# Strassen pairs for blocks 3 and 4 too, and Silu instead of a gated tanh in the pairs: sparse attention and a feed-forward layer on one core

## The chip, the core and the metric

The kernel runs on one core of a Trainium2 chip. The metric is the time of one execution in microseconds of device time, as a median of several runs.

## The reference

Attention in 8 batches of 8 heads, 576 tokens, 64 features each; heads 0 to 3 see the last 32 tokens, heads 4 to 7 every 32nd token. Its output, 4608 tokens of 512 features, goes through a feed-forward layer with silu. All is float32.

```python
scores = q @ k.T / sqrt(64)                     # per batch and head
local   = (rel >= 0) & (rel < 32)               # heads 0..3, rel = i - j
strided = (rel >= 0) & (j % 32 == i % 32)       # heads 4..7
attn = softmax(where(mask, scores, -1e9)) @ v   # (8, 8, 576, 64)
x = attn.transpose(0, 2, 1, 3).reshape(4608, 512)
h = x @ w_in                                    # 512 x 2048
out = (h / (1 + exp(-h))) @ w_out               # 2048 x 512
```

## The kernel before

**Numbers.** Every float32 operand of the feed-forward layer is split into an upper and a lower part in a short float format (fp32r). A product is three matmuls: upper x upper, upper x lower, lower x upper.

**Blocks.** The 4608 tokens are nine blocks of 512, 0 to 8. Block 0 prepares the weights while it computes, by a list written out by hand (PLAN). Block 1 runs plain products in 16 steps. Blocks 2, 3 and 4 (`for k in range(FAST, WIDE_FIRST)`) run the first layer by Strassen's scheme in Winograd's form: in each of eight steps j there are 7 products p1 to p7 of 256 columns instead of 8. Their second layer is plain: four words "0" to "3" in the order of a step stand for the outputs of the step before. Blocks 5 and 6, and 7 and 8, are joined (class `Pair`): two blocks are the two halves of Strassen's scheme, in the first layer (56 products of 512 columns, `first_product`) and in the second (56 more, `second_product`). Here operands are sums of gated values (`sums_before`), each split in two for TensorE (`second_operand`), and results are added up from kept products (`keep`, `finished_out`).

**Sums of weights.** Sums of the weights that the scheme needs are made once, GpSimd for the first layer's (`sum_weights`, in block 1) and VectorE for the second's (`sum_outs`, at the steps in OUT_SUMS, blocks 2 to 4), and kept in DRAM. Products read them through a ring of six, in pairs eight, tiles in SBUF; `stream_on` issues the next load behind the product that frees a tile. All loads and stores of this part are issued by SyncE, in one queue.

**Attention bursts.** The attention of batches 2 to 7 comes in 18 bursts. A burst is two groups, a local and a strided one: TensorE computes the scores of the group after next and the values of this group; then come ScalarE's copies of the values, VectorE's peaks, ScalarE's exps (L529), VectorE's total, scale and transposes, and ScalarE's copies of turned blocks (`turn_across`, L602). The next burst needs what this one has softened. BURSTS says at which step (k, j) one stands. In the blocks a burst holds the four PSUM banks "ps"; in a pair's first layer it takes the banks "po".

**Silu.** Everywhere it is h (1 + tanh(h/2)) / 2: tanh on ScalarE, a `scalar_tensor_tensor` on VectorE for the gating (L1986 in pairs), and the half at the end. Tanh and exp use the same table of ScalarE.

**Order.** From block 1 on, each instruction or small group is a `job` with an engine, a cost, the jobs it follows and the places it takes from rings of buffers. `in_order` gives each job a due time backwards from PE's queue and simulates the engines; PE takes its jobs as written, the other engines choose among the first LOOK jobs, within GRAIN of the earliest start, the one due first. The order found is the program's order on each engine; semaphores make the waits on the chip. The names that the change touches are BURSTS, the orders of words, `job`, `in_order`, `sum_outs`, `burst_jobs`, `finish`, `second_operand`, `sums_before` and `run`; The UNITS (buffers of 128x512 for gated values) and GOPS (places for split operands) lie in SBUF that earlier stages have left.

## Time and profile before

| | us |
|---|---|
| median of 3 runs (820.23 to 820.51) | 820.31 |
| the profiled execution | 824.26 |
| its span, first to last instruction | 822.0 |
| PE matmuls busy | 811.3 (99%) |
| VectorE (DVE) busy | 638.5 (78%) |
| ScalarE (ACT) busy | 557.5 (68%) |
| GpSimd (POOL) busy | 74.3 (9%) |

The mean granted TensorE clock is 0.996 of full speed; it is below only in the slice from 20 to 40 us (0.83). The queue that SyncE issues moves 180.82 MB. A busy time is a union of intervals: two instructions that overlap on one engine count once, and a matmul's end is modelled. Idle time on an engine that nothing waits for costs nothing, so shares alone do not name the bound; the waits and the chain do.

### The profile page before, as it was taken

Reading aid. Unit: us, or ns where it says so; the run is one execution under the profiler, and the core shown is the slowest. Engines: PE = TensorE matmul, PEld = TensorE weight load, DVE = VectorE, ACT = ScalarE, POOL = GpSimd, SP = SyncE. Lnnn points to the kernel's source line nnn. Section 1 sums busy time; section 2 is a strip of 40 time slices with the busy share of each in tenths; the row PEclk is TensorE's granted clock in tenths of the full one; section 3 lists DMA queues with packets and bytes.
Section 4 is the critical chain, followed back from the end, with each engine's and each line's share of the span. In section 5 each row is a group of like instructions: output and inputs, shape, how many; then the busy total and the mean of one; then the engine's idle time right before and its main releaser. Section 6 shows DMA issues by size and latency. Waiting matters only on the chain.

```text
span 822.0 us, 19441 instructions
## 1 busy us (share of the span) xinstructions
PE 811.3 (99%) x7041; PEld 686.5 (84%) x7041; DVE 638.5 (78%) x1571; ACT 557.5 (68%) x1560; POOL 74.3 (9%) x122
## 2 busy tenths in 40 slices
PE   8899999999999999999999999999999999999998
PEld 5688878888898889898988888888888888888887
DVE  6799897787677778786778779676799964789754
ACT  7799876566687678777787769887555624545551
POOL 6300003784000000000000000000000000000000
PEclk9899999999999999999999999999999999999999
DMA  8787354566787876888677877876667697767676
GB/s 270 254 276 253 111 187 127 203 222 237 265 266 252 263 243 210 250 265 264 198 234 247 264 241 242 256 203 181 194 191 219 193 238 227 194 196 194 192 217 156
DMA packets 139007, 182.78 MB, mean 222 GB/s; under 512 B 29408, under 2 KB 82272, under 8 KB 138912
## 3 DMA queue, kind: packets, MB, share of 16 engines
q1 hardware_dynamic: 137392, 180.82, 71.4%
q8 instruction: 56, 0.92, 0.5%
q10 hardware_dynamic: 1520, 0.72, 0.3%
q14 instruction: 39, 0.32, 0.1%
HBM read 142.70 MB, written 38.80 MB: 221 GB/s over the span
## 4 chain that ended last, share of the span: by engine, by line
PE 97%; POOL 1%; issue 1%; DVE 0%; POOLq 0%
PE ps L1549 33%; PE po L779 27%; PE po L2103 13%; PE ps L720 11%; PE ps L2103 4%; PE ps L635 3%; PE po L2232 1%; PE ps L471 1%; PE ps L462 1%; PE po L620 0%; PE po L635 0%; POOL v L399 0%; POOL mask_strided L240 0%; POOL mask__94 L240 0%; PE po L554 0%
## 5 line engine op out<-in xcount | busy, mean ns | idle before, releaser
L1549 PE MATMUL ps<-xop,w 128*128 128x256 f32 (+1 forms) x1152 | 185.5, 310 | 0.0
L1549 PEld LDWEIGHTS ps<-xop,w 128*128 128x128 f32 x1152 | 165.6, 190 | 16.3
L529 ACT ACTIVATE sm<-sm,sums 128x54 f32<-128x54 f32 (+2 forms) x320 | 109.2, 346 | 3.5 <-DVE sums L511 3.4
L720 PE MATMUL ps<-xop,w 128*128 128x512 f32 x384 | 96.5, 400 | 0.0
L1549 PE MATMUL ps<-w,w 128*128 128x512 f32 x384 | 93.7, 389 | 0.0
L779 PE MATMUL po<-w,ghi 128*128 128x512 f32 x280 | 87.1, 392 | 0.0
L720 PEld LDWEIGHTS ps<-xop,w 128*128 128x128 f32 x384 | 72.8, 192 | 15.8
L1549 PEld LDWEIGHTS ps<-w,w 128*128 128x128 f32 x384 | 72.0, 188 | 14.9
L764 DVE TENSOR_TENSOR glo<-th,ghi 128x512 fp32r<-128x512 f32 x80 | 59.3, 743 | 12.4 <-ACT ghi L760 10.5
L529 ACT ACTIVATION_READ_ACCUMULATOR sm<-sm,sums 128x1 f32 x320 | 61.4, 192 | 0.0
L779 PEld LDWEIGHTS po<-w,ghi 128*128 128x128 f32 x280 | 50.4, 189 | 8.9 <-ACT ghi L760 0.2
L760 ACT CAST ghi<-th 128x512 fp32r<-128x512 f32 x78 | 48.3, 621 | 11.8 <-DVE th L752 7.0
L779 PE MATMUL po<-w,glo 128*128 128x512 f32 x140 | 54.6, 390 | 0.0
L779 PE MATMUL po<-stage,ghi 128*128 128x512 f32 x160 | 50.5, 397 | 0.0
L2103 PE MATMUL po<-stage,w 128*128 128x512 f32 x210 | 49.2, 389 | 0.0
L2103 PEld LDWEIGHTS po<-stage,w 128*128 128x128 f32 x210 | 39.4, 188 | 8.2
L602 ACT COPY pt<-sm 32x192 f32<-32x192 f32 (+1 forms) x102 | 36.9, 362 | 5.5 <-DVE sm L594 3.5
L489 POOL MEMSET sm<- 128x80 f32 (+1 forms) x18 | 2.9, 161 | 411.8 <-ACT pt L602 335.0
L1564 ACT ACTIVATE th<-sm 128x512 f32<-128x512 f32 x30 | 18.9, 632 | 29.7 <-DVE sm L1812 24.4
L1942 DVE TENSOR_TENSOR w<-ps,w 128x512 f32<-128x512 f32 x33 | 22.7, 688 | 20.3 <-PE ps L1549 16.3
L2103 PE MATMUL po<-v,w 128*128 128x512 f32 x162 | 38.3, 389 | 0.0
L779 PE MATMUL po<-v,ghi 128*128 128x512 f32 x120 | 38.0, 398 | 0.0
(275 smaller groups left out, 1639.5 us busy)
## 6 DMA issues: line engine op xcount, KB each, us to landing
w<-sums SPq DMA_DIRECT2D x232, 256.0 KB, 3.0
w<-osums SPq DMA_DIRECT2D x104, 256.0 KB, 2.9
sums<-xop SPq DMA_DIRECT2D x16, 512.0 KB, 2.8
osums<-stage SPq DMA_DIRECT2D x16, 512.0 KB, 4.7
v<-vt SPq DMA_DIRECT2D x21, 384.0 KB, 5.3
stage<-w_out SPq DMA_DIRECT2D x14, 512.0 KB, 4.6
k<-kqt SPq DMA_DIRECT2D x14, 477.0 KB, 5.6
stage<-w_in SPq DMA_DIRECT2D x12, 512.0 KB, 4.6
```

What stands on the lines that cost most here:

```text
L462: nc.tensor.matmul(self.pss[h][rows, c * WIDE : (c + 1) * WIDE], kbd[at, 1, g.q0[t] : g.q0[t] + 2 * STRIDE], kbd[at, 0, g.k0[t] : g.k0[t] ...
L529: nc.scalar.activation(out=self.s_sb[:, c, h], in_=self.s_sb[:, c, h], func=AF.Exp, bias=self.peaks[:, c, h : h + 1], scale=-1.0, accum_ou ...
L602: nc.scalar.copy(out=self.pt[to, odd], in_=of)
L635: nc.tensor.matmul(self.pso[p][h * D : (h + 1) * D, i * size : (i + 1) * size], vbd[at, 2 * i + h], moved, start=True, stop=True,)
L720: nc.tensor.matmul(ph, weight(0, wi, fc)[:, cc // 2, cc % 2 * P : (cc % 2 + 1) * P], x[xi][cc], start=(cc, n) == (0, 0), stop=(cc, n) == ( ...
L760: copy[engine](out=g[0][:, cols], in_=th[:, cols])
L764: either[engine].tensor_sub(out=g[1][:, cols], in0=th[:, cols], in1=g[0][:, cols].bitcast(F32))
L779: nc.tensor.matmul(po[tt], g[gi][:, cols], weight(1, wi, fc), start=first and n == 0, stop=last and n == 2,)
L1549: nc.tensor.matmul(bank[:, : right.shape[-1]], left(wi, kt), right[:, kt, xi], start=first and (kt, n) == (0, 0), stop=(kt, n) == (1, 2), ...
L1564: nc.scalar.activation(out=th[:, cols], in_=h, func=AF.Tanh, scale=0.5)
L1942: nc.vector.tensor_add(out=to, in0=of(), in1=to)
L2103: nc.tensor.matmul(bank(name, key, m), left[:, wi, m * P : (m + 1) * P], right[xi], start=first and (j, i) == (0, 0), stop=(j, i) == (FH - ...
```

## The change

WIDE_FIRST goes from block 5 to block 3: blocks 3 and 4 are a pair like 5 and 6. In all pairs ScalarE computes Silu from its own table, straight into the unit, and VectorE's gating goes. In pairs before the last, the result of p3 is copied out of PSUM first, and the sum t1 is made in the first layer. The planner counts a load of the table (1.3 us) where a job needs the other table, lets only one of GpSimd's and VectorE's jobs run where both work on SBUF (port), and counts 1 us more before a store that follows another engine. GpSimd gets three of the eight sums of W2, six sums in each of two pairs, and the turns of three bursts. Bursts move: block 2 has six, pair 3 three in its first layer and three in its second, split around a product. Parts of W1 and W2 are stored in block 1 instead of blocks 2 to 4. The orders of words, LOOK, GRAIN, PASSES and costs are new, and units and split operands have new places.

```diff
-BURSTS = {1: (1, 7, 11), 2: (1, 3, 5, 7), 3: (2, 3, 5, 7), 4: (1, 3, 5, 7), 5: (1, 3, 5)}
-XORDER = ("b21", "b11", "t3", "t2", "b22", "t4", "t1")
-ORDER = "p1 p7 p2 p6 0 p5 1 p4 2 p3 3"
-BURST_ORDER = "0 p1 1 p7 p6 p2 p4 p5 2 3 p3"
-SUPER_LAG = "p1 x x p2 p7 p6 x x p5 p4"
-SUPER_BURST = "p1 p2 p3- p6 p7 B p4 p5"
+BURSTS = {1: (1, 7, 11), 2: (1, 2, 3, 4, 5, 7), 3: (1, 4, 6, "p3:3", "p6:7", "p7:7"), 5: (1, 3, 6)}
+XORDER = ("b11", "t3", "b21", "b22", "t1", "t2", "t4")
+ORDER = "p1 p7 0 p6 p4 1 p2 p5 2 3 p3"
+BURST_ORDER = "B b p1 p7 p6 p2 p4 0 p5 1 2 3 p3"
+SUPER_LAG = "p1 x x x p2 p7 p6 x p5 p4"
+SUPER_BURST = "p1 p7 p2 p3- p6 B p4 p5"
...
-OUT_SUMS = {(2, 2): 0, (2, 4): 1, (2, 6): 2, (3, 2): 3, (3, 4): 4, (4, 0): 5, (4, 2): 6, (4, 4): 7}
+OUT_SUMS = {(2, 0): 7, (2, 2): 1, (2, 4): 3, (2, 7): 5, (3, 1): 2, (3, 4): 4, (3, 5): 0, (3, 6): 6}
-WIDE_FIRST, WIDE_BLOCK = NBLK - 4, NBLK - 2
-KEEPERS = {2: 4, 3: 5}
-UNITS = 35
-EARLY_OUTS = 4
-PASSES = 1
+WIDE_FIRST, WIDE_BLOCK = NBLK - 6, NBLK - 2
+EARLY_KEPT = {at + 7: [(at, 4), (at, 5)] for at in range(8)}
+UNITS = 39
+BETWEEN = 1
+EARLY_OUTS = {0: 0, 1: 1, 2: 2, 4: 4, 6: 6, 14: 3, 3: 7, 9: 5}
+PASSES = 3
...
+TABLE_LOAD = 1.3
+STORE_MARGIN = 1.0
+POOL_OUTS = (0, 1, 2)
+POOL_PAIRS = (3, 5)
+POOL_SUMS = "t1:0 t1:3 t1:5 t4:1 t4:6 t4:7"
+POOL_TURNS = (30, 34, 40)
...
             times = [free[j.engine]]
+            if j.table and j.table != table:
+                times[0] += TABLE_LOAD
+            if j.port:
+                times.append(free["port"])
...
+        by = "POOL" if f in POOL_OUTS else "DVE"
+        add, sub = either[by].tensor_add, either[by].tensor_sub
...
             def curve():
-                th = state["th", (key, name)] = ffn.tile([P, T], F32, name="th", bufs=2)
-                tanh_of(source(), th, slice(0, T))
...
-            g = job("DVE", 0.69, gating, t, ends=t.takes, takes=[] if place else ["unit"])
+                nc.scalar.activation(out=unit(out), in_=source(), func=AF.Silu)
+
+            g = job("ACT", 0.62, curve, made, takes=[] if place else ["unit"], table="silu")
...
+                if self.last:
+                    s[1].takes[0].last.append(self.finish(j, "12", s[3], None))
+                else:
+                    c12, u12 = self.copied("a", j, s[3])
+                    s[1].takes[0].last.append(c12)
+                    g12 = self.finish(j, "12", c12, u12)
+                    g11, u11 = self.gated[j, "11"]
+                    s["t1"] = self.sum_of("t1", j, sub_two, u12, u12, u11, g12, g11)
...
+        def sum_of(self, name, j, op, out, one, two, *after):
+            if self.k in POOL_PAIRS and "%s:%d" % (name, j) in POOL_SUMS:
+                return job("POOL", 1.35, lambda: nc.gpsimd.tensor_sub(
+                    out=unit(out), in0=unit(one), in1=unit(two)), *after)
+            return unit_op(op, out, one, two, *after)
...
+            def products(n):
+                for p, j in itertools.islice(rest, n):
+                    c = plan.get((k, "%s:%d" % (p, j)))
+                    if c is None:
+                        product(p, j)
+                    else:
+                        burst_jobs(c, lambda: [product(p, j), products(BETWEEN - 1)])
...
-    Pair(WIDE_FIRST, False).run(next_operands)
+    for k in range(WIDE_FIRST, WIDE_BLOCK, 2):
+        Pair(k, False).run(lambda k=k: next_operands(k + 2))
```

## Rows read from the trace of the kernel before

**Rows 1.** The page's busy time of TensorE.
```profile
PE 811.3 (99%) x7041; PEld 686.5 (84%) x7041; DVE 638.5 (78%) x1571; ACT 557.5 (68%) x1560; POOL 74.3 (9%) x122
```

**Rows 2.** Waits of PE: for whom, us in total, times, longest; first and last.
```profile
PE po L620 <- issue: 3.2, 2, 2.4
...
PE po L554 <- DVE sm L548: 0.3, 1, 0.3
```

**Rows 3.** Chain that ended last: start us, us, what.
```profile
232.31 1.59 PE po L779 x6
...
324.14 2.87 PE ps L1549 x24
...
334.70 0.66 PE ps L462 x24
...
396.80 1.59 PE po L779 x6
...
490.78 1.59 PE po L779 x6
...
665.65 74.80 PE ps L1549 x330
...
807.09 11.22 PE po L2232 x72
```

**Rows 4.** Stretches: us; busy PE, PEld, DVE, ACT, POOL (counts); clock, DMA share, GB/s.
```profile
131.85:229.00 97.15, 97.15 (x804) 80.11 (x803) 69.52 (x152) 62.93 (x185) 51.47 (x52) 1.00 0.67 229
...
396.80:490.78 93.98, 93.98 (x1050) 84.48 (x1049) 72.60 (x210) 71.73 (x235) 0.65 (x4) 1.00 0.75 246
505.62:588.13 82.51, 82.51 (x673) 68.30 (x673) 59.10 (x136) 61.71 (x158) 0.32 (x2) 1.00 0.70 205
588.13:665.65 77.52, 77.52 (x343) 64.19 (x343) 73.88 (x111) 41.65 (x69) 0.00 (x0) 1.00 0.71 202
...
340.00:360.00 20.00, 20.00 (x243) 18.24 (x242) 16.69 (x55) 18.58 (x73) 0.17 (x1) 1.00 0.93 314
```

**Rows 5.** Groups: line, engine, operation, shapes, count, busy us, mean ns.
```profile
L529 ACT ACT_TABLE_LOAD x1 | 1.3, 1283 | 2.1 <-issue 2.1
...
L1986 DVE SCALAR_TENSOR_TENSOR w<-th,w 128x512 f32<-128x512 f32 x32 | 21.6, 682 | 1.0 <-ACT th L1564 0.9
...
L1332 DVE TENSOR_TENSOR xop<-stage,xop 128x512 fp32r<-128x512 f32 x16 | 14.7, 921 | 6.1 <-ACT xop L1328 5.9
...
L1392 DVE TENSOR_TENSOR stage<-stage 128x512 fp32r<-128x512 f32 x16 | 10.8, 686 | 0.6 <-ACT stage L1388 0.2
...
L1304 POOL TENSOR_TENSOR stage<-w,w 128x512 f32<-128x512 f32 x16 | 25.1, 1592 | 27.9 <-DVE th L752 27.3
...
L1388 ACT CAST stage<-stage 128x512 fp32r<-128x512 f32 x16 | 9.2, 614 | 0.4 <-DVE stage L1384 0.3
```

**Rows 6.** Block 4, ScalarE alone, lines L529, L602, L675 in turn.
```profile
396.80:490.78 93.98, 19.67 (x104) 1.00 0.75 246
...
396.80:490.78 93.98, 11.64 (x32) 1.00 0.75 246
...
396.80:490.78 93.98, 3.74 (x10) 1.00 0.75 246
```

**Rows 7.** Block 4, VectorE alone, lines L511 and L594.
```profile
396.80:490.78 93.98, 4.62 (x49) 1.00 0.75 246
...
396.80:490.78 93.98, 2.83 (x8) 1.00 0.75 246
```

**Rows 8.** ScalarE in time, first and last copy of a burst.
```profile
231.39 0.54 ACT L647 COPY xb<-ps 128x192 f32<-128x192 f32 x2
...
245.67 0.83 ACT L602 COPY pt<-sm 32x256 f32<-32x256 f32 x2
```

**Rows 9.** VectorE in time, the first peak of that burst.
```profile
231.75 0.26 DVE L511 CUSTOM_DVE_ANT_0 sm<-ps,mask 128x96 f32<-128x96 f32 x1 [0.55 <-ACT xb L647]
```

**Rows 10.** DMA issues: names, queue, count, KB each, us to landing.
```profile
w<-sums SPq DMA_DIRECT2D x232, 256.0 KB, 3.0
```

More of the change, by code (lines that the diff above doesn't have):

```diff
@@ L1043, in __init__ @@
             self.after, self.takes, self.late = [j for j in after if j], [], 0.0
-            self.at = self.end = self.due = None
+            self.at = self.end = self.due = self.table = None
     class Place:
@@ L1093, in delay, with job @@
             return 0.0 if a.engine in ("PE", "SP") else 0.03
+        if b.engine == "SP" and a.engine != "PE":
+            return STORE_MARGIN
         return LATENCY.get(a.engine, 0.13 if b.engine == "PE" else 0.07)
-    def job(engine, cost, act, *after, takes=(), ends=()):
+    def job(engine, cost, act, *after, takes=(), ends=(), table=None, port=True):
         made = Job(engine, cost, act, after)
+        made.table = table
+        made.port = port and engine in ("DVE", "POOL") and cost > 0
         made.takes = [Place(rings[name], made) for name in takes]
@@ L1159, in earliest @@
             return max(times)
+        table = "exp"
         while len(order) < len(jobs):
@@ L1172, in in_order @@
                 rings[name].take(n)
+            table = j.table or table
             j.at, j.end = t, t + j.cost
+            if j.port:
+                free["port"] = j.end - LAP.get(j.engine, 0.0)
             free[j.engine] = j.end - LAP.get(j.engine, 0.0)
@@ L1240, in kept_of @@
         if kind != "in":
+            if kind == "out" and which > 3:
+                return [kept_early[f]]
             return [*kept_outs[f], *(kept_outs[f + 1] if kind == "part" else [])]
@@ L1503, in t1 @@
             for cols, (b12, b11) in raw_x(k, size, (0, 1), (0, 0)):
-                nc.vector.tensor_sub(out=sums["t1"][:, :, cols], in0=b12, in1=b11)
+                either[by("t1")].tensor_sub(out=sums["t1"][:, :, cols], in0=b12, in1=b11)
         def sum_of(name, act, n, *before, takes=()):
-            holders[name] = job("DVE", dve(2 * size) + 0.16 * n, act, *before, takes=takes)
+            cost = dve(2 * size) + 0.16 * n
+            engine = by(name)
+            holders[name] = job(engine, cost * (2.2 if engine == "POOL" else 1.0), act, *before, takes=takes)
             return holders[name]
@@ L1531, in operands @@
             makers[name]()
+        for at in range(k * T, k * T + 2 * size, P // 2):
+            x_readers[at // S].extend(ready.values())
         return ready, readers
@@ L1618, in burst_jobs @@
             n = later.g.n
-            each = 0.336 if later.wide else 2 * dve(n * later.seen) / n
-            if not later.g.local and c >= WIDE_FROM:
-                each = 0.62 / n
+            each = 0.62 / n if later.wide else 2 * dve(n * later.seen) / n
+            if later.at_once:
+                each = (0.78 if n == 4 else 0.68) / n
             peaks = []
@@ L1630, in burst_jobs @@
                 for c_ in range(n):
-                    exps.append(job("ACT", each, lambda a=later, c=c_, h=h: a.weigh([c], [h]), peaks[h]))
+                    exps.append(job("ACT", each, lambda a=later, c=c_, h=h: a.weigh([c], [h]), peaks[h],
+                                    table="exp"))
             soft.append((i + 2, later, peaks[0], exps))
@@ L1915, in sparse_attention_ffn, with old_places_end @@
     unit_places = {}
-    xjobs, xplaces = made[WIDE_FIRST]
-    for place, last in zip(old["unit"], (
-        [[final[1]]] * 3 + [list(xjobs.values())] * 5 + [lag_outs] * 14 + [[g1l]] + [last_bursts] * 12
-    )):
-        place.last = last
+    def old_places_end():
+        for place, ends in zip(old["unit"], unit_ends):
+            place.last = [*ends()]
+        for i, place in enumerate(old["gop"]):
+            own = i < OWN_GOPS
+            place.last = lag_outs + freed[NFC - OWN_GOPS + i] if own else last_bursts
     def unit(place):
@@ L2141, in act @@
                     )
-            out["place"].last.append(job("SP", (4, 256), act, *after))
+            out["place"].last.append(job("SP", (4, 480), act, *after))
         def keep(self, which, name, made):
```

245 lines of the change are left out of this document (142 added, 103 removed).

## The prediction

> **What bounds the kernel now.** I read the busy times first: TensorE's matmuls fill 811.3 of the profile's 822.0 us [rows 1]. A busy PE need not be an efficient one, so I went on to PE's own waits. They come to about 7 us in six entries, all from the start and the attention of the first block; the first and the last entry stand in [rows 2]. So from about 30 us on PE never waits, and the chain of waits must be a list of PE work in program order, which it is [rows 3]. Hence each product taken out of PE's queue shortens the kernel by its own length, until another engine becomes late. The reader is to see two things in rows 3: that stages have a fixed length that can be added up, and that there is no idle piece between them. The busy times by stage (block 1, block 4, the two layers of pair 5 and a busy slice, [rows 4]) then show how much room VectorE and ScalarE have where work is moved to. They are at 72.6 and 71.7 us of 93.98 in a single block with four bursts, but VectorE is at 73.9 of 77.5 us in the second layer of a pair.
>
> **PE's work, part by part.** A single block without bursts is eight steps (j) of 7 half-width products and 4 outputs. One such step runs from 324.14 to 334.70, 10.56 us [rows 3]. A block with four bursts takes 490.78 - 396.80 = 93.98 us, so a burst costs (93.98 - 8 x 10.56) / 4 = 2.38 us. In a pair, 55 products of the last first layer take 74.80 us, 1.36 us each, and a pair has 56 + 56 = 112 of them: 152.3 us. The check: 665.65 + 152.3 = 818.0, and the last piece ends at 807.09 + 11.22 = 818.3 [rows 3]. Blocks 3 and 4 therefore go from 2 x 84.5 = 169.0 us to 152.3 us: **-16.7 us**. The 18 bursts stay 18, at the same 2.38 us, three of them still in block 1 and three in pair 5. Only the places of the others move: block 2 gets six and pair 3 gets six. The startup, its fixed plan and the last products stay.
>
> **Silu in pairs.** Each pair has 32 tanh with 32 gatings on VectorE at 0.68 us [rows 5]; the gating goes and Silu stands in tanh's place, which I take at tanh's length. PE waits for neither in a first layer, because the gated values are read only in the second. This frees 32 x 0.68 = 21.8 us of VectorE per pair, and the sum of PE changes by nothing. Silu and exp need a switch of ScalarE's table. The trace of before has one load, 1.28 us [rows 5]. With three bursts between Silus in a first layer that is two switches a burst, 6 x 1.28 = 7.7 us. First layer of pair 3 on ScalarE, from that of pair 5: 61.7 [rows 4] + 7.7 + eight more copies of c12 and eight for 4 sums of W2 (0.61 each, [rows 5], 9.8) - 2 x 2.9 for the turns of two bursts that go to GpSimd (11.64 us for four bursts, [rows 6]) = 73.4 of 82.5 us, 89%. That holds, so I take 0 for it. Bounds: 0, and what a Silu that runs short of units would cost, one product of 1.36 us per burst, 4.1 us.
>
> The Trainium skill (ScalarE: Activation LUTs, "What ACT_TABLE_LOAD costs") says that each switch to another set costs the load and a drain of about 1380 ns, 2.66 us in all, and that calls should be batched by set. The load in the row agrees with its 1283 ns; no run here shows the drain. By that price ScalarE's first layer would be at an estimated 81.7 of 82.5 us, which speaks against exp among Silus, and then the 0 above would be 1 or 2 us.
>
> **Block 2 with six bursts.** A burst's softmax takes 37.2 / 4 = 9.3 us of ScalarE (four lines, three of them in [rows 6]) and 26.5 / 4 = 6.6 us of VectorE (eight lines, the first and the last in [rows 7]). Block 2 now has 84.5 + 6 x 2.38 = 98.8 us of PE and 71.7 + 2 x 9.3 + 1.1 (one more sum of W2) = 91.4 us of ScalarE, 93%; VectorE 72.6 + 13.2 + 1 = 86.8 us, 88%. The bursts stand at j = 1, 2, 3, 4, 5, 7, so four gaps are only one step long: 10.56 + 2.38 = 12.94 us. ScalarE's share of such a gap is 9.3 + (71.7 - 37.2) / 8 = 13.6 us. It is short by 0.67 us, and PE waits for it through the copies of the products and through the next burst's softmax. Four gaps: **+2.7 us**. Lower end: operands and sums of W2 are postponed past j = 5, then ScalarE's share is below 12.94 and the loss is 0. Upper end: the softmax of a burst isn't quicker than now. It begins at the burst's end, 232.31 [rows 3], and its last turn ends at 245.67 + 0.83 = 246.50 [rows 8], 14.2 us later. The next burst would then come every 14.2 + 2.38 = 16.6 us, 3.6 us late, 14.6 us in four gaps. I take 2.7, near the low end: in those 14.2 us ScalarE also did other copies, since the next burst was two steps, 2 x 10.56 + 2.38 = 23.5 us, off, and the plan sorts by due times.
>
> **The order behind a burst.** In block 2 p1 follows at once, where an output of 1.39 us stood between. The bursts hold all four ps banks. The local scores' peaks begin at 231.75 [rows 9], and six of them at 0.18 us free the first bank near 232.3 and the second near 232.9; PE was done with the burst at 232.31. So p1 waits some 0.1 us, plus 0.1 for the semaphore: 0.2 us a burst, six bursts, **+1.2 us**. Below: 0. Above: ScalarE, busier, brings the copy ahead of the peaks one instruction later (0.6 us), 0.8 x 6 = 4.8 us.
>
> **Second layer of pair 3.** VectorE: 73.9 [rows 4] + 3 x 6.6 for the bursts at p3:3, p6:7 and p7:7, less the eight t1 made in the first layer (5.5) and three t4 on GpSimd (2.1) = 86.1 us, against PE's 77.5 + 3 x 2.4 = 84.7. Short by 1.4 us. The burst at p3:3 finds d in two of the four ps banks, so its second half waits for its own first half beyond the product between them: its first copy starts at 231.39 [rows 8] and its peaks end near 232.9, 1.5 us and some 0.2 for PE's end before it; the product takes 1.36, which leaves 0.4 us. Together **+1.8 us**. Below: 0, since outputs and operands can slide into the next first layer, which lost its gatings. Above: if all of the last burst and of pair 5's operands must be done where they stand, some 3.5 us more, 5.3.
>
> **GpSimd, stores and loads.** Three of the eight sums of W2, 12 sums and three bursts' turns go to GpSimd, at 1.35 us for 128x512 in the plan. In before, 16 subtractions of VectorE that meet GpSimd's work take 921 ns where 16 others of that shape take 686, and GpSimd's own take 1592 [rows 5]. The new plan lets only one of the two run. Either way it is some 0.24 us per meeting, in first layers where VectorE has room (59.1 of 82.5 us, less 21.8 of gatings): 0, at most 2 us.
>
> The Trainium skill (GPSIMD Engine Reference, "1. Specifications") gives the reason for such meetings: the two engines share SBUF interfaces when VectorE reads two SBUF inputs; its advice to keep elementwise work on VectorE would undo these moves. Row and rule agree, and the sum by it is the same.
>
> Loads: pair 3 streams 112 x 0.26 = 29.4 MB, with six bursts' k and v (1.5 MB each by their tiles), four sums and the outputs (1 MB each) some 45 MB in 167 us, 270 GB/s. A stretch of before moved 314 GB/s without a wait of PE [rows 4], and a weight load lands in 3.0 us [rows 10] where the ring is eight products, 10.9 us, ahead. Stores of W1 parts go to block 1, which moves 229 GB/s over its length [rows 4] and gets 7.3 MB more, 304 GB/s: near that 314, but PE's operands there are resident. Cost 0; upper end 3 us, two products late in each of the tight stretches.
>
> **Sum.** The profiled execution takes 824.26 us, 822.0 of it span; the median is 820.31, 3.95 below. Nothing of the change lies outside the span. 824.26 - 16.7 + 2.7 + 1.2 + 1.8 = 813.3 by the profile's own time, and 820.31 - 11.0 = **809.3 us** as a median.
>
> **Rivals.**
> (A) No new stall: everything moved finds room. For it: before hides VectorE at 95% in a second layer with no wait of PE [rows 4]. Against: no gap of before is as tight as 12.94 us. Time 820.3 - 16.7 = 803.6.
> (B) ScalarE and VectorE saturate: upper ends of the bank wait (4.8), of the second layer (5.3) and half of the softmax's excess (4 x 0.9). 803.6 + 13.7 = 817.3. For it: 93% and 102% are computed from full loads; against: work can slide past both stages.
> (C) Slower: the softmax becomes a chain that sets the pace. Its place is the four gaps of block 2 and the one from p6:7 to p7:7 (10.9 + 2.4 = 13.3 us). With ScalarE at 93% instead of 76% it stretches, 14.2 x 93 / 76 = 17.4 us, so a gap takes 19.8: 4 x 6.9 + 6.5 = 34 us, 838 us. It decides from 16.7 / 5 = 3.3 us a gap, which is today's 14.2 us unshortened. Against it: the chain has only 9.3 us of ScalarE in it.
> (D) A table switch that holds ScalarE longer than its load. Were it twice the 1.28 us of [rows 5], that is 7.7 us more in the first layer of pair 3 and of pair 5 each, and ScalarE comes to 98% in the first; copies that free PE's banks come late, and I let a fifth of the 15.4 us reach PE: 812.3. For it: a burst's exps come in two halves, so there may be more than two switches. Against: PE waits for no Silu. The Trainium skill's 2.66 us a switch, cited above, is this rival.
>
> **Chances.** Forecast with (D), 805.5 to 812.5: 0.62, of which (D) 0.08. (A), below 805.5: 0.17. (B), 812.5 to 818.6: 0.12. Between 818.7 and 821.9, within 0.2% (1.6 us, about what a measurement tells from no change): 0.03. (C), above: 0.06. So faster 0.91, same 0.03, slower 0.06. The range 803.5 to 816 leaves out most of (C), the upper part of (B) and little else.
>
> **What would show it.** The new pair's 112 products at 1.36 us in the chain; waits of PE for ScalarE and VectorE in block 2's steps 1 to 5, 4 us in all; ScalarE above 90% there; loads of the table in the first layers of pairs 3 and 5, some 14, with no PE wait beside them; no gating in pairs; VectorE above 95% in pair 3's second layer. It is wrong if PE waits for a weight load, if PE's waits exceed 12 us behind block 1, or if pair 3 needs more than 172 us with its six bursts and the last outputs of block 2.

## The result and the profile after

The changed kernel takes 812.88 us (median of 5 runs, 811.85 to 814.05) where the kernel before takes 820.31 us (819.82 to 821.86): 0.9901 of it, 95% interval 0.9886 to 0.9915. It is 7.4 us faster; 809.3 was forecast, 11.0 us faster. The profiled executions stand 10.2 us apart (814.05 with a span of 812.3 us, and 824.26 with 822.0).

The busy times of the changed kernel, the row that answers to [rows 1]:

```profile
PE 798.4 (98%) x6657; PEld 661.1 (81%) x6657; DVE 605.0 (74%) x1469; ACT 573.0 (71%) x1539; POOL 115.6 (14%) x176
```

384 matmuls fewer, VectorE less busy, ScalarE and GpSimd more. TensorE still fills the span, so the rows to read next are its waits, as in [rows 2]: for whom, us in total, times, longest.

```profile
PE ps L479 <- DMA k<-kqt: 2.7, 4, 1.2
PE po L479 <- issue: 1.6, 1, 1.6
...
PE ps L1582 <- ACT ghi L768: 1.0, 4, 0.3
...
PE ps L1582 <- ACT xq L1841: 0.4, 2, 0.2
PE ps L643 <- DVE th L1592: 0.4, 2, 0.2
```

The first line belongs to the start. The lines that name ghi, xq and th are new: all eight waits lie in block 2, and they sum to 1.8 us. The stretches of the changed kernel, in the columns of [rows 4]: block 2 from its first burst to pair 3's first product, the two layers of pair 3, the two of pair 5.

```profile
229.43:321.44 92.01, 90.07 (x1248) 80.91 (x1248) 78.72 (x248) 80.67 (x288) 6.76 (x11) 1.00 0.79 260
321.44:409.01 87.57, 87.57 (x748) 72.65 (x747) 61.98 (x158) 71.90 (x199) 18.77 (x29) 1.00 0.84 269
409.01:495.33 86.32, 86.30 (x736) 70.57 (x735) 77.37 (x169) 69.03 (x178) 8.52 (x11) 1.00 0.79 240
495.33:578.38 83.05, 81.48 (x667) 67.28 (x667) 50.87 (x123) 67.80 (x173) 7.53 (x13) 1.00 0.75 219
578.38:655.90 77.52, 77.52 (x344) 64.19 (x343) 65.28 (x98) 40.05 (x66) 4.68 (x3) 1.00 0.72 204
```

TensorE is idle for 1.9 us of block 2 and for 1.6 us of pair 5, and nowhere else here. Block 2's bursts cost 92.01 against 7 x 10.56 + 6 x 2.38 = 88.2 us, 3.8 more; pair 3, which also holds the last four outputs of block 2, takes 173.9 against 152.3 + 6 x 2.38 + 4 x 1.39 = 172.1 us, so 1.8 more. The 55 products in a row of the last pair are untouched ("655.90 74.80 PE ps L1582 x330" in the chain, 74.80 as in [rows 3]).

The groups that answer to [rows 5]: table loads, Silu, one of the subtractions that met GpSimd, GpSimd's sums.

```profile
L537 ACT ACT_TABLE_LOAD x5 | 6.4, 1283 | 2.8 <-issue 2.2 <-DVE sums L519 0.6
L2062 ACT ACT_TABLE_LOAD x5 | 6.4, 1283 | 0.1
...
L2062 ACT ACTIVATE w<-w 128x512 f32<-128x512 f32 x43 | 26.6, 631 | 11.5 <-DVE w L2024 11.1
...
L1354 DVE TENSOR_TENSOR xop<-stage,xop 128x512 fp32r<-128x512 f32 x16 | 12.0, 763 | 6.1 <-ACT xop L1350 6.1
...
L1326 POOL TENSOR_TENSOR stage<-w,w 128x512 f32<-128x512 f32 x16 | 22.5, 1426 | 27.7 <-DVE th L760 27.2
```

Ten loads of 1.28 us where one stood; the gating's 682 ns rows are gone.

### The profile page after: what moved, and what is told of

Its sections match the earlier page's. It is cut to its first block, busy times and chain, and to the rows that moved or that the text cites. A ratio compares the mean times of both kernels' runs of the same rounds, so it can differ in the third digit from the quotient of the medians.

```text
span 812.3 us, 18695 instructions
## 1 busy us (share of the span) xinstructions
PE 798.4 (98%) x6657; PEld 661.1 (81%) x6657; DVE 605.0 (74%) x1469; ACT 573.0 (71%) x1539; POOL 115.6 (14%) x176
## 4 chain that ended last, share of the span: by engine, by line
PE 92%; DMA 3%; ACT 3%; DVE 1%; issue 1%; SPq 0%; ACTq 0%; DVEq 0%
PE ps L1582 33%; PE po L2186 20%; PE po L787 15%; PE ps L728 10%; PE ps L2186 7%; DMA k<-kqt 2%; PE ps L643 2%; PE po L2329 1%; PE ps L479 1%; DMA sums<-xop 1%; PE ps L470 1%; PE po L643 1%; ACT ghi L768 1%; PE po L470 0%; PE po L479 0%
## 5 line engine op out<-in xcount | busy, mean ns | idle before, releaser
L1582 PE MATMUL ps<-xop,w 128*128 128x512 f32 (+1 forms) x720 | 144.9, 348 | 1.6 <-ACT ghi L768 1.0
L1582 PE MATMUL ps<-w,w 128*128 128x512 f32 x576 | 138.6, 390 | 0.0
L1582 PEld LDWEIGHTS ps<-xop,w 128*128 128x128 f32 x720 | 117.5, 189 | 20.7 <-ACT ghi L768 1.4
L1582 PEld LDWEIGHTS ps<-w,w 128*128 128x128 f32 x576 | 107.8, 188 | 22.5 <-DMA w<-sums 0.2
L2186 PE MATMUL po<-stage,w 128*128 128x512 f32 x456 | 107.0, 390 | 0.0
L2186 PEld LDWEIGHTS po<-stage,w 128*128 128x128 f32 x456 | 85.2, 188 | 17.9 <-DVE stage L2166 0.2
L728 PEld LDWEIGHTS ps<-xop,w 128*128 128x128 f32 x384 | 72.0, 190 | 15.4
L787 PE MATMUL po<-w,ghi 128*128 128x512 f32 x168 | 52.1, 392 | 0.1
L2162 ACT CAST stage<-w 128x512 fp32r<-128x512 f32 x49 | 30.4, 622 | 19.4 <-DVE stage L2166 10.3
L2166 DVE TENSOR_TENSOR stage<-w,stage 128x512 fp32r<-128x512 f32 x49 | 35.1, 723 | 11.6 <-ACT stage L2162 11.1
L2186 PE MATMUL ps<-stage,w 128*128 128x512 f32 x168 | 39.4, 391 | 0.0
L2186 PEld LDWEIGHTS ps<-stage,w 128*128 128x128 f32 x168 | 31.4, 188 | 6.6
L768 ACT CAST ghi<-th 128x512 fp32r<-128x512 f32 x46 | 28.3, 622 | 8.6 <-DVE th L760 5.5
L2020 ACT COPY w<-ps 128x512 f32<-128x512 f32 x46 | 26.7, 585 | 10.7 <-PE ps L1582 9.8
```

The lines of the kernel that those rows point to most:

```text
L728: nc.tensor.matmul(ph, weight(0, wi, fc)[:, cc // 2, cc % 2 * P : (cc % 2 + 1) * P], x[xi][cc], start=(cc, n) == (0, 0), stop=(cc, n) == ( ...
L768: copy[engine](out=g[0][:, cols], in_=th[:, cols])
L787: nc.tensor.matmul(po[tt], g[gi][:, cols], weight(1, wi, fc), start=first and n == 0, stop=last and n == 2,)
L1582: nc.tensor.matmul(bank[:, : right.shape[-1]], left(wi, kt), right[:, kt, xi], start=first and (kt, n) == (0, 0), stop=(kt, n) == (1, 2), ...
L2020: copy_ps(out=unit(place), in_=of())
L2162: copy_ps(out=gated_ops(to.slot)[0], in_=unit(place))
```

## Where the 3.8 us of block 2 are

TensorE in time, behind the second burst of block 2, with the idle time before an instruction and who ended it in brackets:

```profile
242.98 0.73 PE L470 MATMUL ps<-k 64*64 64x96 f32 x24
...
245.54 1.67 PE L1582 MATMUL ps<-xop,w 128*128 128x256 f32 x12 [0.20 <-ACT ghi L768]
247.42 2.41 PE L1582 MATMUL ps<-xop,w 128*128 128x256 f32 x18 [0.21 <-ACT xq L1841]
```

The first burst of block 2 in the kernel before, and what follows it:

```profile
229.96 0.73 PE L462 MATMUL ps<-k 64*64 64x96 f32 x24
...
232.24 0.73 PE L779 MATMUL po<-k,ghi 128*128 128x512 f32 x2
```

And the chain of waits in the changed kernel:

```profile
244.95 0.52 ACT ghi L768
245.47 0.52 ACT stage L1412
...
246.35 0.80 ACT xb L683 x3
247.15 0.22 ACT xq L1841
247.42 2.41 PE ps L1582 x18
```

p1 starts at 245.54. The profile names a cast of ScalarE (ghi, L768) that ends at 245.47; the peaks of the burst, which free p1's bank, are at work there too, and which of the two holds p1 is not shown. p7 follows, and p6 at 247.42 waits for the copy of p1 (xq, L1841), which stands on ScalarE behind two casts, exponentials and three copies of the burst's values. Only p7 lies between p1 and p6.

The listed idle time is 1.9 us, half of the 3.8. It counts from the modelled end of the matmul before; the starts show the whole. From a burst's first scores to its first product the kernel before takes 2.16 to 2.28 us (229.96 to 232.24 above), the changed kernel 2.55 to 2.79 (242.98 to 245.54): some 2.6 us in six bursts. The 12 matmuls of p1 and p7 take 1.88 us from 245.54 to 247.42 where 12 x 0.12 = 1.44 would do ([rows 3], 2.87 us for 24); with what follows p6 that is 0.3 to 0.5 us behind four of the bursts, some 1.6 us. So these two places hold all of it.

Is it ScalarE's load? It is busy 80.67 of 92.01 us of block 2, 88%, but 50.63 of 54.26 us, 93%, of the four tight gaps (sums over the four, and the one gap of the kernel before that is one step long, in its block 3):

```profile
sum 54.26, PE 53.04 PEld 47.49 DVE 46.37 ACT 50.63 POOL 6.57; mean PE 13.26 PEld 11.87 DVE 11.59 ACT 12.66 POOL 1.64
```

```profile
334.63:347.53 12.90, 12.90 (x196) 11.70 (x195) 10.15 (x37) 11.56 (x45) 0.00 (x0) 1.00 0.87 259
```

The kernel before has ScalarE at 90% of such a gap and no wait; there an output stands behind the burst, and another between p1 and p7. The share alone does not tell load from order; two runs below do. Twice, by the profile, the burst's own values wait 0.19 us for a gating of block 2's products on VectorE (th, L1592), not for the softmax.

## The experiments

All runs stand beside the kernel before on the same chip; its median there was 820.9 to 821.9 us, and single runs spread over 6 to 8 us. So the whole time resolves about 2 us, and the stretches between the bursts are read from each profile. This table gives them (us from the first scores of one burst to those of the next, the matmuls of L470 in TensorE's timeline): the four tight gaps of block 2; its last gap; to pair 3's burst at step 1; from there to step 6; on to p3:3; to p6:7; from p6:7 to pair 5's first burst. Rows that begin with a quotation mark are the row above with one more edit. The changed kernel and the control are the same kernel, and their rows agree to 0.02 us. Two stretches outside the table do not repeat like this: from block 1's last burst to block 2's first these two took 34.94 and 34.38 us, and between the first two bursts of pair 5 21.58 and 22.45.

```
kernel                 tight gaps of block 2     last  to p.3  1-6    6-p3:3 p3:3-p6:7  p6:7-pair 5
changed                13.55 13.70 13.22 13.79   24.39 33.71   52.51  41.84  19.62      54.45
control                13.54 13.71 13.23 13.79   24.40 33.71   52.49  41.84  19.62      54.45
0, 1 moved up          13.14 13.41 13.07 17.59   23.98 34.52   52.49  41.84  30.06      54.45
0 before p6            13.22 13.23 13.44 13.31   24.07 34.59   52.55  41.84  30.29      54.45
 ", cheap table        13.22 13.22 13.31 13.32   24.07 34.62   53.47  45.25  19.62      54.45
turns on GpSimd        13.63 14.83 13.40 14.87   25.35 33.81   52.49  41.84  29.50      54.45
stores earlier         13.57 13.73 13.23 13.80   24.41 33.72   52.49  41.84  19.62      54.45
unsplit                13.54 13.71 13.22 13.79   24.40 33.71   52.51  41.84  19.52      54.92
pass put back          13.56 13.71 13.21 13.80   24.39 33.71   52.52  41.84  29.25      54.45
 ", cheap table        13.54 13.71 13.22 13.78   24.41 34.40   53.29  48.29  19.64      54.45
 ", due exps           13.56 13.72 13.23 13.79   24.41 33.72   52.51  43.28  20.69      54.73
ports not apart        13.54 13.71 13.23 13.81   23.87 34.25   52.49  41.91  19.38      54.45
```

**The control**, nothing edited.

> The changed kernel itself, nothing edited, beside the kernel before on one chip. The runs with one order or place changed (the cover moved, more turns on GpSimd, the early stores) came out 8 to 14 us above the 812.9 us of the changed kernel's own runs. Theory: they lose that by what was edited, each in one or two places of the plan, and the control gives 812 to 814 us, 0.988 to 0.992 of before, with the bursts of block 2 spaced 13.2 to 13.8 us as before. Rival: part of it belongs to the chip that they ran on; then the control stands at 818 to 822 us, 0.997 to 1.000 of before.

812.15 us (808.99 to 817.2), 0.9886 [0.9858, 0.9914]. The gain is there beside other runs of the kernel before, and its gaps are those of the changed kernel to 0.02 us. So what the edited kernels lose in those gaps comes with their edits.

**Blocks 3 and 4 single again.** The places of the bursts, the orders of words and the steps of the sums of W2 are those of before (their lines are left out below), and GpSimd makes no turns; the rest of the change is kept.

```diff
-BURSTS = {1: (1, 7, 11), 2: (1, 2, 3, 4, 5, 7), 3: (1, 4, 6, "p3:3", "p6:7", "p7:7"), 5: (1, 3, 6)}
+BURSTS = {1: (1, 7, 11), 2: (1, 3, 5, 7), 3: (2, 3, 5, 7), 4: (1, 3, 5, 7), 5: (1, 3, 5)}
...
-WIDE_FIRST, WIDE_BLOCK = NBLK - 6, NBLK - 2
+WIDE_FIRST, WIDE_BLOCK = NBLK - 4, NBLK - 2
...
-POOL_PAIRS = (3, 5)
+POOL_PAIRS = (5,)
```

> The changed kernel with blocks 3 and 4 single again: WIDE_FIRST, the places of the bursts, the steps of the sums of W2 and the orders of words are those of before; Silu in the two pairs, the port, store and table rules of the planner, the early stores and the new buffers stay. If the whole gain comes from PE's 16.7 us fewer, as predicted, this kernel takes what before took, 820.3 within 1.5 us, since no stage of before waited for VectorE or ScalarE. Rival: Silu and the planner gave part of the 7.4 us; then it is below 818.

822.35 us, 1.0004 [0.9984, 1.0025]. Silu in pair 5, the plan's rules and the stores are all in it and give nothing that can be measured. The busy times:

```profile
PE 811.7 (99%) x7041; PEld 686.2 (83%) x7041; DVE 590.9 (72%) x1483; ACT 565.1 (69%) x1571; POOL 98.2 (12%) x146
```

TensorE is back at the 811.3 us of [rows 1]; VectorE is 47.6 us below [rows 1] and that gains no time. Within the interval the whole gain is TensorE's work on fewer products.

**Two products moved up behind the bursts of block 2.**

```diff
-BURST_ORDER = "B b p1 p7 p6 p2 p4 0 p5 1 2 3 p3"
+BURST_ORDER = "B b 0 p1 p7 1 p6 p2 p4 p5 2 3 p3"
```

> The changed kernel with one edit: in block 2's steps with a burst the first output stands between the burst and p1, and the second between p7 and p6, as in the order of before. In the changed kernel block 2 takes 92.0 us from the start of its first burst to the first product of pair 3, where 88.2 would do by 7 x 10.56 + 6 x 2.38; it loses 3.8 us behind its six bursts. Theory 1, the order: p1 follows a burst at once and waits for its PSUM bank, and p6 waits for the copy of p1, with one product of 0.72 us between. Then this kernel's block 2 takes 88.2 to 89.5 us and its time is 2.5 to 3.8 us below the changed kernel's 812.9, about 809.7. Theory 2, ScalarE's throughput: 13.6 us of ScalarE stand against 12.94 us of PE in each tight gap; then the wait only moves, to an output that waits for its operand or to the next burst that waits for its softmax, block 2 stays at 91.5 to 92.5 us, and the time at 812 to 814.

826.65 us, 1.0059 [1.0038, 1.0081]: slower than before, and neither theory's time. In the table three tight gaps got 0.16 to 0.40 us shorter, as the waits of p1 and p6 say. The fourth got 3.8 us longer: there the turns were late, the values waited 2.0 us, and the granted clock was 0.50 for 3.4 us behind that wait. And a place that the edit does not touch, pair 3's burst at p3:3, cost 10.4 us. That event decided four of the twelve runs, so it is told once, below.

**One product moved, between p7 and p6.**

```diff
-BURST_ORDER = "B b p1 p7 p6 p2 p4 0 p5 1 2 3 p3"
+BURST_ORDER = "B b p1 p7 0 p6 p2 p4 p5 1 2 3 p3"
```

> One output product (0) is moved between p7 and p6 of the tight gaps of block 2, so that 1.4 us more of TensorE lie between p1 and p6, which waits for a copy of p1 on ScalarE. Theory: the waits of p6 (0.2 us in each gap) go, those of p1 behind the burst stay, and block 2 from its first burst to pair 3 falls from 92.0 to about 91 us; the rest stays, 811.5 to 812 us if the control is at 812.9. Rival: the gaps are short of ScalarE (88% busy), not of cover: the 0.2 us turns up elsewhere in the gap and the bursts stay 13.2 to 13.8 us apart. A third way, seen when two products were moved: the plan puts a softmax later, the values of one burst wait 2 us or more for its turns, and pair 3's p3 burst waits up to 8 us; then 818 us or more.

822.37 us, 1.0005 [0.9987, 1.0023]. The four tight gaps sum to 53.20 against 54.27 us, 1.07 less, the next is 0.33 shorter, and the way to pair 3 is 0.88 longer: 0.5 us net. The waits for xq are gone from block 2. The theory on the order holds with half its size, the third way came too.

**More turns on GpSimd** (block 2's too).

```diff
-POOL_TURNS = (30, 34, 40)
+POOL_TURNS = (18, 20, 22, 24, 26, 28, 30, 34, 40)
```

> The changed kernel with one edit: the turns of the softmax (the copies of L610) of block 2's six bursts are made by GpSimd, like those of three later bursts, which takes some 2.9 us a burst, 17 us in all, off ScalarE (80.7 us busy in block 2's 92.0). Theory 2, ScalarE's throughput: the tight gaps get 10.7 us of ScalarE for 12.94 us of PE, and block 2 falls to some 89 us, time about 810. Theory 1, the order behind a burst: the copies that p1 and p6 wait for stand among exps and copies of values, not among turns; block 2 stays within 1 us of 92.0, time 812 to 814. If GpSimd's turns lie longer in the softmax's chain, the next burst waits for it and block 2 becomes longer than 92.5.

826.73 us, 1.0057 [1.0036, 1.0078]. ScalarE gave up 11 us (561.8 us busy against 573.0) and block 2 got longer, not shorter: two tight gaps are 1.1 us longer and the last gap 0.95, since p6 waits for p1's copy:

```profile
PE ps L643 <- POOL pt L610: 7.6, 1, 7.6
PE ps L1582 <- ACT xq L1841: 3.8, 3, 1.3
```

ScalarE's share of the four tight gaps fell from 93% to 70% (39.90 of 56.73 us). Had its throughput been short, the gaps would have shrunk. What counts is which instruction stands ahead of that copy: at 247.75, in the second gap, five exponentials and the copies of the values. The first row is the event at p3:3 again.

**The W1 stores seven steps earlier.**

```diff
-EARLY_KEPT = {at + 7: [(at, 4), (at, 5)] for at in range(8)}
+EARLY_KEPT = {at: [(at, 4), (at, 5)] for at in range(8)}
```

> The changed kernel with one edit: the stores of W1's parts 4 and 5 (16 stores of 256 KB) are issued in steps 0 to 7 of block 1 instead of steps 7 to 14. From the last burst of block 1 to the first of block 2 the changed kernel takes 34.94 us, before took 34.04, and in that stretch a store of a sum took 8.4 us to land. Theory 3, the stores: they fill the DMA engines (89% of block 1, before 67%), the sum's place in xop comes free late, and operands of block 2 with it. Then the stretch falls back to 34.0 to 34.3 us and the time by 0.6 to 0.9, about 812.1. Rival: the new order of ScalarE's and VectorE's work at the end of block 1 makes the outputs' operands late, whatever the stores do: the stretch stays at 34.7 to 35.2 us and the time at 812.9.

822.69 us, 1.0014 [0.9993, 1.0036]. Behind block 1 every stretch is the control's; block 1 lost 7.0 us between its second and third burst (31.48 against 24.51) and 1.4 to 2.6 to block 2 (36.30 against 33.7 to 34.9 where the edit lies behind block 1). Neither the theory nor its rival had this. How it comes about, ScalarE and VectorE in time:

```profile
174.85 0.62 ACT L1350 CAST xop<-stage 128x512 fp32r<-128x512 f32 x1 [4.40 <-DMA sums<-xop]
...
175.89 0.53 ACT L655 COPY xb<-ps 128x192 f32<-128x192 f32 x2
176.24 0.26 DVE L519 CUSTOM_DVE_ANT_0 sm<-ps,mask__97 128x96 f32<-128x96 f32 x1
...
177.00 3.32 PE L728 MATMUL ps<-xop,w 128*128 128x512 f32 x7 [2.94 <-DVE sums L519]
```

And a stretch in the columns of [rows 4]:

```profile
175.80:182.60 6.80, 5.60 (x13) 4.46 (x14) 4.85 (x20) 4.37 (x23) 5.75 (x7) 0.50 0.54 176
```

The store that frees an xop buffer lands late behind those moved ahead of it. The cast into that buffer holds ScalarE's queue for 4.40 us, the burst's copies and peaks stand behind it, and TensorE waits 2.94 us for a bank. The granted clock is at half for 6.8 us, from 175.8 on. So the late place of these stores is worth 8 to 10 us in this order, and the estimate "cost 0" for them was right only with it.

**The second-layer bursts whole.**

```diff
-burst_jobs(c, lambda: [product(p, j), products(BETWEEN - 1)])
+if p == "p3":
+    burst_jobs(c, lambda: [product(p, j), products(BETWEEN - 1)])
+else:
+    burst_jobs(c)
+    product(p, j)
```

> The second-layer bursts of p6 and p7 in the pairs stand whole in front of their product again; the one of p3 stays split around it. Theory: each split costs a second change of the matmul shape of 0.2 to 0.25 us and nothing else, so pair 3 gets 0.4 to 0.5 us shorter (173.9 to 173.4 us) and the whole 812.5 us, a difference at the edge of what five rounds show. Rival: the product between the halves covers the peaks and exponentials of the local group; without it the values wait for the softmax, 0.5 to 1 us at each of the two, and the whole is 1 to 2 us longer than the control.

812.75 us, 0.9891 [0.9869, 0.9913], no difference from the control. The table: 0.47 us longer from p6:7 on and 0.10 shorter before it. By its starts a split does cost: the product between the halves takes 1.59 us and not 1.36 in each of the three bursts of the changed kernel. But without the two splits TensorE waits twice, 0.6 us by the profile, for VectorE's operands of the second layer (stage L2166), and the starts there are over 0.4 us late each time. In all the split pays 0.37 us more than it costs. The rival's wait of the values for the softmax is not in the list.

**GpSimd and VectorE not kept apart in the plan.**

```diff
-            if j.port:
-                times.append(free["port"])
```

> The changed kernel whose plan no longer keeps GpSimd's and VectorE's work on SBUF apart (one rule of its plan taken out; everything else as it is). Theory: GpSimd is busy 14% of the span, so few of VectorE's passes meet it; those that do last 0.92 and not 0.69 us; TensorE's time stays within 1 us of the control (812.2). Rival 1: the slowed passes stand in the softmax and split chains of the tight gaps, and blocks 1 and 2 get 2 to 5 us longer. Rival 2: keeping them apart costs more than the contention, since VectorE and GpSimd wait for each other in the plan; then the kernel is 1 to 2 us faster than the control.

815.27 us (811.34 to 818.14), 0.9911 [0.9890, 0.9932]; the intervals of the ratio overlap with the control's, so this stays open within 3 us. A stretch of block 1 is 0.82 us longer (25.33 against 24.51), and those of block 2 and pair 3 move by up to 0.54 us both ways. The profiled run, 818.14 us, is the longest of the six; it holds a wait of 2.6 us in pair 5 with 6.8 us at half clock around it. Waits in that place come and go (see below). The subtractions of L1354 take 795 ns without the rule and 763 with it, against 921 before [rows 5]: most of that difference is not the rule's.

## One event, seven runs: who stands behind a table load

Pair 3's burst at p3:3 (scores at 436.78), in the kernel with 0 and 1 moved up. TensorE and ScalarE in time:

```profile
436.78 0.73 PE L470 MATMUL ps<-k 64*64 64x96 f32 x24
445.08 1.90 PE L643 MATMUL ps<-pt,v 64*64 64x32 f32 x48 [7.58 <-POOL pt L610]
```

```profile
391.58 1.28 ACT L2062 ACT_TABLE_LOAD   x1
...
437.53 1.28 ACT L537 ACT_TABLE_LOAD   x1
438.82 0.38 ACT L537 ACTIVATE sm<-sm,sums 128x96 f32<-128x96 f32 x1
```

These exponentials belong to the burst before, whose scores stand at 394.94. In the changed kernel that burst's scores stand at 394.30 and its exponentials begin at 397.06; here they begin at 438.82, behind the scores of the next burst. Between them ScalarE did Silus, casts and copies. The reason can be read in the plan: a job whose table isn't loaded starts 1.3 us later in its eyes (TABLE_LOAD), and it takes the most urgent only among jobs that start within 0.2 us of the first (GRAIN). While any other job of ScalarE is ready, an exponential behind Silu's table is never chosen, however overdue. In the changed kernel the exp table happens to be in place before that burst:

```profile
384.14 1.28 ACT L537 ACT_TABLE_LOAD   x1
385.43 0.38 ACT L537 ACTIVATE sm<-sm,sums 128x96 f32<-128x96 f32 x1
...
407.26 1.28 ACT L2062 ACT_TABLE_LOAD   x1
```

What the wait costs, in three stretches of the kernel with 0 and 1 moved up (columns as in [rows 4]):

```profile
426.00:437.51 11.51, 11.50 (x72) 9.17 (x70) 9.20 (x14) 5.63 (x9) 1.66 (x1) 1.00 0.68 200
437.51:445.08 7.57, 0.00 (x0) 0.00 (x0) 7.03 (x16) 6.16 (x29) 2.63 (x4) 0.75 0.42 111
445.08:451.50 6.42, 6.42 (x118) 5.20 (x118) 5.17 (x20) 2.59 (x11) 3.13 (x6) 0.50 0.50 160
```

7.57 us of idle TensorE, in which the clock falls to half, and then 6.42 us of work at half clock (1.2 GHz), 3.2 us lost: 10.8 in all, against 30.06 - 19.62 = 10.4 in the table. Four kernels show it, with 9.6 to 10.7 us each. The next four runs ask whether the plan's price of a table load is the cause, or VectorE.

**The gating's pass put back on VectorE.**

```diff
-            out = place or placed(g.takes)
+            silued = g
+
+            def again():
+                nc.vector.scalar_tensor_tensor(
+                    out=unit(out), in0=unit(out), scalar=1.0, in1=unit(out), op0=ALU.mult, op1=ALU.max,
+                )
+
+            g = job("DVE", 0.69, again, silued)
+            out = place or placed(silued.takes)
```

> Behind each Silu one VectorE pass in place over its 128x512 tile is put back (maximum of the value with itself; the result is unchanged), as long as the gating product that Silu replaced: 32 x 0.69 = 22.1 us of VectorE in each of the pairs 3 and 5. Theory: VectorE is not what bounds the first layers (62 of 87.6 us in pair 3, 51 of 83.1 in pair 5), and TensorE's time stays within 1 us of the control. Rival: Silu's relief of VectorE is what lets pair 3 run at TensorE's pace; then pair 3 gets 4 to 10 us longer, TensorE waiting for splits and casts, and half or all of the change's gain is gone.

820.78 us, 0.9997 [0.9977, 1.0017]: by its time the rival's case, the whole gain gone. By its stretches not. First control, then this kernel: pair 3's burst 1 to 6, 6 to p3:3, p3:3 to p6:7.

```profile
339.95:392.44 52.49, 52.49 (x475) 43.61 (x474) 34.41 (x92) 43.52 (x119) 11.68 (x18) 1.00 0.90 293
392.44:434.28 41.84, 41.84 (x303) 34.71 (x302) 31.06 (x67) 31.52 (x77) 6.58 (x10) 1.00 0.79 247
434.28:453.90 19.62, 19.60 (x209) 15.82 (x208) 18.82 (x49) 16.58 (x52) 3.12 (x4) 1.00 0.89 263
```

```profile
340.24:392.76 52.52, 52.52 (x475) 43.57 (x474) 47.45 (x107) 44.16 (x120) 13.76 (x18) 1.00 0.88 277
392.76:434.60 41.84, 41.84 (x303) 34.69 (x302) 37.11 (x72) 26.31 (x48) 3.89 (x2) 1.00 0.84 266
434.60:463.85 29.25, 21.68 (x210) 17.34 (x209) 27.31 (x67) 22.41 (x82) 7.61 (x12) 0.82 0.64 177
```

With 13 us more of VectorE in the first stretch and 6 in the second, both are as long as the control's. Only the third differs, by the event: ScalarE did 5 us less in the second and began the exponentials in the third.

**The same, the plan counting a table load as 0.19 us.**

```diff
-TABLE_LOAD = 1.3
+TABLE_LOAD = 0.19
```

> As the kernel with the gating's pass put back on VectorE, but the plan counts a change of ScalarE's table as 0.19 us and not 1.3, so that an exponential no longer stands behind every Silu, cast and copy that could start without a load. With 1.3 that kernel stood at 820.8 us: the exponentials behind pair 3's burst before p3's were put off by 40 us, the values of p3's burst waited 7.6 us and the clock fell to half for 10.2 us. Theory: those 9.6 us come from the order alone and VectorE has room for the pass; the burst before p3's and the next stand 19.6 us apart again and the time is 812 to 814.5 us, although ScalarE loads its tables some ten times more (12.8 us of ScalarE). Rival: the 22.1 us of VectorE in each pair are what is missing; then TensorE waits spread over the pairs and the time stays at 817 to 821 us.

819.79 us, 0.9982 [0.9966, 0.9998]. The event is gone (19.64), and the time hardly moves: the stretch before it got 6.45 us longer. There the chain of waits is ScalarE's:

```profile
408.07 1.28 ACT L537
409.37 1.40 ACT sm L537 x8
410.79 1.28 ACT L2062
412.08 0.63 ACT w L2062
412.73 1.28 ACT L537
```

Eight loads, 10.3 us, stand in this stretch, one in the control's (in the expectation of the last run below I wrote five of them; it is eight). One Silu, one load, eight exponentials, one load: a plan that thinks loads free changes tables at every chance. My theory missed by 5 us. The time is the rival's, but its reason isn't: the waits stand in one stretch, behind the loads.

**One product moved, table load at 0.19 us.**

> Product 0 between p7 and p6 in block 2, as before, with the plan's table change at 0.19 us. With 1.3 the four tight gaps between bursts were 13.22, 13.23, 13.44 and 13.31 us against 13.54, 13.71, 13.23 and 13.79 in the control (1.07 us less), the last two stretches 0.55 us more, and pair 3's p3 burst cost 10.7 us. Theory: the gaps of block 2 keep their 13.2 to 13.4 us, the 10.7 us go, and the time is 0.3 to 1.2 us under the control's 812.2, some ten more table loads being hidden under TensorE. Rival: the exponentials come in time but the loads (12.8 us more of ScalarE in pair 3) delay splits and casts; then pair 3 is 2 to 6 us longer than the control's and the time is 813.5 to 818 us.

816.05 us, 0.9945 [0.9923, 0.9966]. Block 2 keeps its short gaps, the event is gone, and pair 3 loses 3.4 us before p3:3 with six loads in that stretch and 1.0 us before: the rival's case. With the pass on VectorE and eight loads it was 6.45.

**The pass put back, the load at 1.3 us, and an exponential due within 2 us may be taken.**

```diff
-firsts.append(min((f for f in found if f[0] <= start + GRAIN), key=lambda f: f[1].due))
+firsts.append(min((f for f in found if f[0] <= start + GRAIN or f[1].table == "exp" and f[1].table != table
+                   and f[0] - TABLE_LOAD <= start + GRAIN and f[1].due <= start + 2.0), key=lambda f: f[1].due))
```

> As the kernel with the gating's pass put back on VectorE, the plan's table change at 1.3 us again; one rule added: an exponential whose due time is less than 2 us off may be taken although its table has to be loaded first. So neither are the exponentials put off by 40 us (820.8 us, 10 table loads) nor do the tables change at every chance (819.8 us, 20 loads, of which five stood in the stretch that got 6.4 us longer). Theory: both losses are of the plan's tables and VectorE has room for its 22.1 us in each pair; about 12 loads, no stretch of pair 3 more than 1.5 us longer than the control's, no half clock at p3's burst, and 812 to 815 us. Rival: VectorE's passes are what is missing; then pair 3's first layer or the stretch before p3's burst is 4 us or more longer, with VectorE busy over 90% of it, and the time is 817 us or more.

813.83 us (811.24 to 815.78), 0.9908 [0.9886, 0.9931]: the gain is back although VectorE does all the passes that Silu had taken from it. 12 loads; the stretches before and behind p3:3's burst are 1.44 and 1.07 us longer than the control's, with VectorE at 90% of the first:

```profile
390.27:433.55 43.28, 42.18 (x304) 34.62 (x303) 38.89 (x79) 32.92 (x78) 7.60 (x10) 1.00 0.82 256
```

So Silu's relief of VectorE is worth 0 to 3 us here, and the order of the exponentials about 7 us (820.78 to 813.83). The rule was tried on this one of the four kernels with the event, and not on the changed kernel. No edited kernel beat the changed one: the short gaps of block 2 (0.5 us) never came without a price in pair 3.

## Why the prediction came out as it did

**PE's work, -16.7: right.** The chain has the new pair's products at the same 1.36 us, and with blocks 3 and 4 single again TensorE's busy time and the kernel's time are those of before.

**Block 2, +2.7 and +1.2: the size right (3.9 against 3.8), by luck, for the first mechanism is wrong.** I had ScalarE short by 0.67 us a gap. It is 93% busy in the tight gaps, as the sum said, but taking 11 us off it shortened nothing, and one product moved took 1.07 us from the four gaps with its work unchanged (50.42 against 50.63 us). The step that held is the order behind a burst, and it was sized at less than half: by the starts p1 is late by some 2.6 us in six bursts, not 1.2, and p6, which I did not look at, by some 1.6 for p1's copy. Between p1 and p6 lies one product. The trace of before spoke against the first term already. Against (A) I wrote that no gap of before is as tight as 12.94 us; one is, 12.90 us in its block 3, without a wait, and the softmax of the burst ahead of it was done 10.6 us behind that burst (its last turn ends at 347.43, the burst at 336.79). So the 14.2 us of my upper end, and of (C), were no lower limit.

**Pair 3's second layer, +1.8: the size right, again partly by luck.** VectorE's short-fall did not come (77.37 of 86.32 us, 90%, where I had 86.1; no wait of PE). Counted with products of 1.36 us, its three split bursts cost 3.30, 2.75 and 2.82 us against 2.38 (stretches of 19.62, 13.63 and 25.94 us with 12, 8 and 17 products), and that is 1.7 of the 1.8 us. The second half of p3:3's burst takes 0.45 us longer than those of the other two (1.42 against 0.97 and 0.96 us), which is the wait that I had at 0.4; the rest is the split, some 0.4 us in each, of which 0.23 lies in the product between the halves. It stands where I had put VectorE's 1.4. One of my signs of being wrong came true: pair 3 needs 173.9 us, more than 172. But that bound stood below my own sum, 152.3 + 14.3 + 5.6 + 1.8 = 174.0.

**Silu and its tables, 0: right for this order alone.** 10 loads and not some 14, and no PE wait beside them. A load takes 1.28 us and the next exponential begins at its end (384.14 and 385.43 above). The Trainium skill (ScalarE: Activation LUTs, "What ACT_TABLE_LOAD costs") adds a drain of about 1380 ns to each switch; in no row here does it show (the copy ahead of that load ends at 384.12), so rival (D) had no ground in that price. But tables had a price of another kind, which none of my cases had: they decide when exponentials start. Put off, one burst cost 10 us; changed too often, a stretch cost 6.4.

**Rival (C), the softmax as a chain: its mechanism is real, and 0.06 was fair only for this one order.** A burst's softmax that came late decided five of the edited kernels (four by the event at p3:3, one of them by a gap of block 2 as well; the early stores by a cast ahead of its copies in the queue). At p3:3 it came from the order that a plan chose, not from ScalarE's load as I had derived it.

**What the sum lacked.** By the profiles I forecast 824.26 - 11.0 = 813.3 us and got 814.05. From block 2's first burst to the end of the last product the profile of before takes 588.35 us and that of after 579.13: 9.2 less, where my terms give 11.0. Of the 1.8 us between them 1.6 are one wait in pair 5 (issue, PE po L479). Six of the twelve kernels with the new pair have it there, at 0.7 to 2.6 us, and six have not; the kernel before and the one with single blocks have not. Whether it belongs to the change stays open. Ahead of block 2 the two profiles differ by 0.9 us (34.94 against 34.04, the stretch that does not repeat) and by -1.4 us in the start: the first scores of block 1's first own burst stand at 131.3 to 136.0 us in the executions here, at 135.9 in that of before and 134.4 in that of after.

The medians lie 7.4 us apart, 3.6 less than forecast. The profiled execution of before stood 3.95 us over its median and that of after 1.17, and I carried a difference of profiles over to the medians. How much of these excesses is the start is not shown, with one profile of each. By the control's ratio the gain is 9.4 us (7.1 to 11.7). So 812.88 lies 0.4 us above the band that I gave 0.62, in the band of (B), and the control's 812.15 just inside the first; (B)'s mechanism, two engines that saturate, is not what the runs show.

## What to carry to other kernels

Where one engine fills the span, count the work that leaves its queue, and then what comes back in each tighter gap: here some 0.6 us a burst, through the order of a few instructions and not through an engine's load. A planner's price for a table load wants a rule for due times beside it: here, priced alone, it let one class of work stand until it was late, and nearly unpriced it changed tables at every chance. And when an edit in one place moves the whole time, compare the stretches between fixed landmarks before believing that the edit did it: four of these runs lost 10 us at one burst, in three of them well behind the places that were edited.

## What the runs showed of the hardware

The granted clock fell to 0.50 (1.2 GHz) in stalls that were short against the span: within the idle stretches of 7.57 us, for 6.8 us around waits of 2.94 us (the early stores) and 2.6 us (ports not apart), and for 3.4 us behind a wait of 2.0 us (0 and 1 moved up, block 2); a wait of 2.1 us in pair 5 (turns on GpSimd) left it at 1.00. The 6.42 us of work behind the first ran at half clock, so that a wait of 7.57 us cost 9.6 to 10.7. In the kernel whose waits were cut into pieces (4.5 us in all of the 48.3 us before p3:3, the longest 1.6) the clock stayed at 1.00.
